# Attention bias rows loaded earlier into four tiles, and zero fills moved to middle units

## The chip, the core and the metric

The kernel runs on one core of a Trainium2 chip. It drives five engines: PE (matmuls, with its weight loads PEld), DVE (vector), ACT (scalar), POOL (GpSimd) and SP, which here issues nearly all transfers in program order; 16 DMA engines carry them. The metric is the device time of one execution in microseconds (us), the median of several runs.

## The reference

Three stages in float32: attention with a bias that depends on the distance of two positions, a gated feed-forward layer, and a layer of eight experts of which each token goes to one.

```python
# attention: batch 2, 8 heads, 576 positions, 64 per head
scores = scale * np.matmul(q, k.transpose(0, 1, 3, 2))
x = (psi_rel / psi_i)[..., None]          # log1p(|i-j|) / log1p(max(i,1))
bias = np.maximum(x @ w1 + b1, 0.0) @ w2  # hidden 32, one bias per head
scores = scores + bias.transpose(2, 0, 1)[None]
scores = scores - np.max(scores, axis=-1, keepdims=True)
attn = np.exp(scores); attn = attn / (np.sum(attn, -1, keepdims=True) + 1e-09)
x = np.matmul(attn, v)                    # then reshaped to 1152 x 512
# feed-forward: 512 -> 1536 -> 512
x = (silu(x @ w_gate) * (x @ w_val)) @ w_out
# experts: argmax routing, at most 288 tokens each, 512 -> 1024 -> 512
y = np.maximum(disp @ w1, 0.0) @ w2
out[i] = gate_w[i] * y[expert_idx[i], pos[i]]
```

## The kernel before

The attention part works in 36 *units*. The 576 query rows are cut into four chunks of 128, taken from the middle outwards, and one of 64 at the end. Each full chunk c has eight units, one for each pair of heads p and batch b, with b the fastest; the last chunk has four (units 32 to 35), one for each pair of heads, with the 64 rows of both batches side by side. One unit makes the scores of two heads ("halves"): PE multiplies queries and keys into the PSUM tile `ps_s` (line L189); DVE adds the bias and takes the row minimum of the negated sum in one instruction per half (L206, "softmax" below); ACT takes the exponential (L214); POOL adds a small number to the sums (L220), DVE inverts them (L223), POOL normalises (L227); PE transposes the weights (L256 and L262), ACT and DVE copy them out of PSUM (L267, L272, L274); PE multiplies with the values (L286), and ACT and DVE split the result into a high and a low part (L302, L304). These steps are spread over four turns of one loop: turn u does unit u's softmax, most of unit u-1's transposes, unit u-3's value product, and the scores of unit u+1. Within a turn their order is a written list (`ORDER`; `LATE` from turn 25, `TAIL` from turn 35).

The bias is made on the chip in groups of 16 query rows. DVE makes the clipped distances `bt` (L110), PE multiplies them (L128), ACT scales the result into `bo` (L146, L153), and SP stores it to the DRAM tensor `bias_d` (L157). Eleven groups are made ahead of the loop; turn u makes group 11+u (counted in the order in which the chunks are taken), until turn 24. In turns 13 to 16 and 21 to 24 a piece of that product is put in the unused half of a bank of the current unit's first score tile (`MR`), as soon as the softmax has read it.

`load_bias` (L162) fetches the bias of one chunk and one pair of heads from `bias_d` into an SBUF tile `bias_sb`: three transfers (L168 to L170), or six for the last chunk, whose rows are fetched once for each batch. A tile serves the two batches of one pair, so two units; in the last chunk it serves one. There are three such tiles in turn. The loads are issued at the head of a turn (`loads`); a load must wait until the stores of the rows that it reads have landed and until the units that used its tile are through their softmax.

SP issues everything in program order, and an instruction that waits holds all behind it. At the head of a turn stand the loads of bias, keys, values and queries, then raw weights for the next layer (turns 18 to 22), then zero fills; the group's store comes late in the turn, after ACT has written it. The zero fills are 12 transfers that clear the dispatch buffer (9 of them, `disp`) and the output (3), both in DRAM, from one SBUF tile `zero`, which POOL sets to zero once (`late["idle"]`, L603). They are issued one per turn by `late["zero"]` (L520). The feed-forward layer after the attention begins in the last three turns.

Of the kernel before, what the change touches and what calls it, by code (L numbers as in the profile page):

```python
# [10 lines left out]
F32 = mybir.dt.float32  # L11
# [26 lines left out]
LEAD = 11  # L38
IDLE = (26, 12)
RAW0 = 18  # L40
JOB0 = 25
GEO0 = 400


def attention(tc, ident, shape, qd, kd, vd, wb, geo, xh, xl, late):
    nc = tc.nc
    B, H, S, D = shape
    P = 128
# [14 lines left out]
    with ExitStack() as ctx:  # L63
        cst = ctx.enter_context(tc.tile_pool(name="a_cst", bufs=1, side="right"))
        io = ctx.enter_context(tc.tile_pool(name="a_io", bufs=2, side="right"))
# [21 lines left out]
        def load_k(b, p):  # L87
            nc.sync.dma_start(kst[:, b * NP + p], kd[b * NP + p])

        def load_v(p):  # L90
            nc.sync.dma_start(vn[:, p].rearrange("p b c d -> p (b c d)"), vd[:, p])
# [3 lines left out]
        def load_q(t):  # L95
            qst[t] = io.tile([P, NP, P], F32, tag="qst", name="qst", bufs=5)
            nc.sync.dma_start(qst[t].rearrange("p h i -> p (h i)"), qd[t])
# [61 lines left out]
        bias_sb = {}  # L159

        def load_bias(c, p):
            t = io.tile([P, 2, S], F32, tag="bias", name="bias_sb", bufs=3)  # L162
            for i0, p0, n in ([(c * P, 0, P)] if c < NF else [(c * P, 0, LO), (c * P, LO, LO)]):
                def rows(j, j0, w):
                    w_ = H * PITCH - 1
                    o = i0 * w_ + I16 - 1 + (2 * p + j) * PITCH + j0
                    return bd[o:o + n * w_].rearrange("(i w) -> i w", w=w_)[:, :w]
                nc.sync.dma_start(t[p0:p0 + n, 0, :], rows(0, 0, S))  # L168
                nc.sync.dma_start(t[p0:p0 + n, 1, LO:], rows(1, 0, NF * P))
                nc.sync.dma_start(t[p0:p0 + n, 1, :LO], rows(1, NF * P, LO))  # L170
            bias_sb[c, p] = t

        order = sorted(range(NF), key=lambda c: abs(2 * c + 1 - NT_))
        units = [(c, p, b) for c in order for p in range(NP) for b in range(B)]
# [37 lines left out]
        def exp(u, j):  # L212
            e, (mn, sm) = e_t[u], st_t[u]
            nc.scalar.activation(  # L214
                e[:, j, :], e[:, j, :], AF.Exp, bias=mn[:, j:j + 1], scale=-1.0, accum_out=sm[:, j:j + 1]
            )
# [8 lines left out]
        def normalise(u, j):  # L225
            e, rs = e_t[u], rs_t[u][:, j:j + 1]
            nc.gpsimd.tensor_scalar(e[:, j, :], e[:, j, :], rs, 1.0, ALU.mult, ALU.mult)  # L227
# [36 lines left out]
        def t_evac(u, part):  # L264
            et, ps = et_t[u], tp_t[u, part]
            if part == 2:
                nc.scalar.copy(et[:, (NB_ - 1) * P:], ps)  # L267
                return
            dst = et[:, :(NB_ - 1) * P].rearrange("p (n i) -> p n i", i=P)[:, :, part * HP:(part + 1) * HP]
            src = ps.rearrange("p (n i) -> p n i", i=HP)  # L270
            if part == 1:
                nc.vector.tensor_copy(dst, src)  # L272
            else:
                nc.scalar.copy(dst, src)  # L274
# [40 lines left out]
        def early_raw(n, h):  # L315
            r = io.tile([P, S], F32, tag="knat", name="raw0", bufs=4)[:, :512].bitcast(I32)
            late["load"](n, h, r)
            raw0.append((n, h, r))

        def early_steps(n, h, r):  # L320
            t, g = (wk.tile([P, S], F32, tag="bt", name="dec0", bufs=12)[:, :256] for _ in range(2))
            spare.append([*zip("ADDDDAD", late["decode"](n, h, r, t.bitcast(I32), g))])
# [20 lines left out]
        with tc.manual_schedule():  # L343
# [47 lines left out]
            def loads(u):  # L391
                qc = order[u // 8 + 1] * B if u // 8 < NF else None
                for x in range(3, NU):
                    if units[x][2] in (0, None) and u == max(x - 2, x // 8 * 8 - 1, 0):
                        load_bias(*units[x][:2])
                if u + 4 < len(korder):
                    load_k(*korder[u + 4])
                if u % 2 == 0 and 0 < u // 2 + 1 < NP:
                    load_v(u // 2 + 1)
                if u % 4 == 0 and qc is not None:  # L400
                    load_q(qc + u % 8 // 4)

            for u in range(NU + 2):
                if u < NU:
                    loads(u)
                if u in (RAW0, RAW0 + 1):
                    for h in range(2):
                        early_raw(u - RAW0, h)
                if u in (RAW0 + 2, RAW0 + 4):
                    late["load1"]((u - RAW0) // 2 - 1)  # L410
                if u == RAW0 + 4:
                    late["idle"]()
                if u > RAW0 + 4:
                    late["zero"]()
                if u == NU - 1:
                    dec1 = [late["decode1"](n, *(
                        wk.tile([P, S], F32, tag="bt", name="dec1", bufs=12)[:, :512].bitcast(d) for d in (I32, F32)
                    )) for n in range(2)]
                if u == JOB0:
                    for x in raw0:  # L420
                        early_steps(*x)
                R, ahead = (groups[n] if n < NG else None for n in (LEAD + u, LEAD + u + 1))
                todo = [] if ahead is None else list(range(4))

                steps = {
                    "T": (1, transposes),
                    "T9": (1, transpose_last),
                    "V0": (1, lambda v: t_evac(v, 0)),
                    "V1": (1, lambda v: t_evac(v, 1)),
                    "V2": (1, lambda v: t_evac(v, 2)),  # L430
                    "S0": (0, lambda v: softmax(v, 0)),
                    "S1": (0, lambda v: softmax(v, 1)),
                    "E0": (0, lambda v: exp(v, 0)),
                    "E1": (0, lambda v: exp(v, 1)),
                    "A": (0, add_eps),
                    "R": (0, recip),
                    "N0": (1, lambda v: normalise(v, 0)),
                    "N1": (1, lambda v: normalise(v, 1)),
                    "AV": (2, av),
                    "Q": (-1, qk),  # L440
                    "XH": (2, lambda v: evac(v, 0)),
                    "XL": (2, lambda v: evac(v, 1)),
                }
                bias = {
                    "MR": lambda: bias_mm(R, 1, {1: s_ps[u, 0][:, 1, HS:]}),
                    "M": lambda: bias_mm(R, 0),
                    "BE": lambda: bias_evac(R, 0),
                    "BR": lambda: bias_evac(R, 1),
                }
                for name in TAIL[u - NU + 1] if u >= NU - 1 else LATE if R is None else ORDER:  # L450
                    if name == "B":
                        if todo:
                            t4 = todo.pop(0)
                            bias_t4(ahead, t4, t4 + 1)
                    elif name in ("JD", "JA"):
                        job(u, name[1])
                    elif name == "JJ":
                        turn = NU
                        while any(spare):
                            job(turn, "D")  # L460
                            job(turn, "A")
                            turn += 1
                    elif name in ("K0", "K1"):
                        dec1[int(name[1])].pop(0)()
                    elif name in ("G0", "G1"):
                        gate0(int(name[1]))
                    elif name == "ACT":
                        nc.scalar.activation(ncst, ncst, AF.Sigmoid)
                    elif name in bias:
                        if R is not None:  # L470
                            bias[name]()
                    else:
                        name, _, back = name.partition(":")
                        default, step = steps[name]
                        v = u - int(back or default)
                        if 0 <= v < NU and (name, v) not in ran:
                            ran.add((name, v))
                            step(v)
                if u == NU + 1:
                    late["act"]((psg[0], psg[1]), wk.tile([P, S], F32, tag="bt", name="sg0", bufs=12))  # L480
                    for steps in dec1:
                        for step in steps:
                            step()
# [943 lines left out]
```

## Time and profile before

| | |
|---|---|
| median of 3 runs (lowest, highest) | 529.27 us (528.96 to 529.32) |
| the profiled execution | 528.89 us, of which the span is 527.2 us |
| attention, from the start to the last units | about 0 to 165 us of the span |
| PE busy, share of the span | 501.4 us, 95% |
| DVE busy | 370.1 us, 70% |
| ACT busy | 267.6 us, 51% |
| POOL busy | 104.0 us, 20% |
| HBM traffic over the span | 169 GB/s mean |

The span is what the profiler recorded from the first to the last instruction. Busy time of PE counts modelled ends of pipelined matmuls, so a busy PE may still be waited for or waiting in small parts; idle time that a row gives in brackets, with the releaser behind an arrow, is time in which the engine had nothing that it could start. The granted clock is the part of TensorE's full clock that the chip gave in a stretch. DMA share is the mean busy share of the 16 DMA engines; it can pass 1.00 a little in a short stretch. The slices of the page (40 of 13.2 us each) look like this over the attention part, the first 13 digits of each line:

```
PE   7999999999997
DVE  6899999997976
DMA  7896645779974
```

### The profile page before, as it was taken

The numbers are of one execution on the slowest core, as the hardware profiler recorded it, in microseconds if no ns is written. First come the engines' busy times: TensorE is split into PE (matmuls) and PEld (weight loads), VectorE is DVE, ScalarE is ACT, GpSimd is POOL, SyncE is SP. The second block draws the span as 40 slices with busy tenths as digits, with TensorE's granted clock in tenths as the row PEclk, the third lists the DMA queues.
The fourth block names the chain that finished last, engine by engine and source line by source line (L and its number), as shares of the span: only waits on it lengthen the run. The fifth ranks groups of instructions, "written<-read, shape, count | busy, mean of one in ns | idle before, by whom it ended". The sixth has DMA issues, their size and how long they took to land. (4 is left out here: it accounts for less than half of the span.)

```text
span 527.2 us, 11901 instructions
## 1 busy us (share of the span) xinstructions
PE 501.4 (95%) x4348; PEld 412.5 (78%) x4348; DVE 370.1 (70%) x931; ACT 267.6 (51%) x583; POOL 104.0 (20%) x218
## 2 busy tenths in 40 slices
PE   7999999999997999999999999999999599999685
PEld 4467666667767999978999889999777588897554
DVE  6899999997976899996799827643456555646221
ACT  5798889898865445453633203522323254437200
POOL 1055444444551100000000000000032210602213
PEclk9999999999998999999999999999999699999999
DMA  7896645779974754353231000000016699936720
GB/s 256 282 366 229 199 139 180 234 225 327 284 225 151 245 202 145 110 192 113 80 121 40 2 0 1 1 1 1 0 51 241 240 365 404 375 122 208 261 109 9
DMA packets 49937, 88.82 MB, mean 168 GB/s; under 512 B 7954, under 2 KB 27412, under 8 KB 49856
## 3 DMA queue, kind: packets, MB, share of 16 engines
q1 hardware_dynamic: 48416, 84.78, 47.7%
q0 software_dynamic: 1296, 3.03, 1.5%
q8 instruction: 40, 0.66, 0.5%
q14 instruction: 41, 0.34, 0.2%
q10 hardware_dynamic: 144, 0.02, 0.0%
HBM read 66.73 MB, written 22.15 MB: 169 GB/s over the span
## 5 line engine op out<-in xcount | busy, mean ns | idle before, releaser
L566 PE MATMUL ps_gv<-xh,hl 128*128 128x384 f32 x528 | 135.0, 336 | 0.0
L566 PEld LDWEIGHTS ps_gv<-xh,hl 128*128 128x128 f32 x528 | 95.5, 188 | 0.1
L566 PE MATMUL ps_gv<-xl,hl 128*128 128x384 f32 x264 | 88.7, 336 | 0.0
L859 PE MATMUL ps_o<-hl,hh 128*128 128x512 f32 x216 | 73.0, 404 | 0.2 <-ACT y L864 0.2
L214 ACT ACTIVATE e_sb<-e_sb,mn 128x576 f32<-128x576 f32 x72 | 55.4, 771 | 5.6 <-DVE mn L206 5.2
L206 DVE CUSTOM_DVE_ANT_0 e_sb<-ps_s,bias_sb 128x576 f32<-128x576 f32 x72 | 52.0, 754 | 8.8 <-DMA bias_sb<-bias_d 6.3
L227 POOL TENSOR_SCALAR e_sb<-e_sb,rs 128x576 f32<-128x576 f32 x72 | 55.2, 778 | 13.3 <-DVE rs L223 12.9
L110 DVE TENSOR_SCALAR bt<-geo_sb 128x320 f32<-128x320 f32 (+17 forms) x144 | 57.4, 439 | 0.0
L650 POOL DMA_INDIRECT disp<-y,rsi x9 | 9.0, 999 | 223.8 <-DVE rs L807 207.3
L566 PEld LDWEIGHTS ps_gv<-xl,hl 128*128 128x128 f32 x264 | 49.6, 188 | 0.1
L859 PEld LDWEIGHTS ps_o<-hl,hh 128*128 128x128 f32 x216 | 40.6, 188 | 10.4 <-issue 1.4
L286 PE MATMUL ps_x<-et,vn 128*64 128x128 f32 (+1 forms) x800 | 48.4, 271 | 0.2
L189 PE MATMUL ps_s<-kst,qst 64*128 64x288 f32 (+1 forms) x320 | 45.9, 426 | 0.0
L286 PEld LDWEIGHTS ps_x<-et,vn 128*64 128x64 f32 x800 | 40.2, 141 | 3.4 <-DVE xl L304 0.4
L576 ACT CAST hh<-sg 128x384 fp32r<-128x384 f32 x36 | 18.4, 511 | 47.7 <-DVE sg L575 47.7
L859 PE MATMUL ps_o<-hl,hlo 128*128 128x512 f32 x105 | 42.0, 400 | 0.0
L549 ACT CAST hl<-dg 128x512 fp32r<-128x512 f32 x32 | 19.1, 620 | 39.5 <-PE ps_o L859 21.6
L189 PEld LDWEIGHTS ps_s<-kst,qst 64*128 64x128 f32 (+1 forms) x320 | 24.8, 175 | 10.5 <-DVE mn L206 1.4
L256 PEld LDWEIGHTS ps_t<-ident,e_sb 64*128 64x128 f32 x576 | 24.3, 141 | 9.4 <-DVE et L272 3.1
L575 DVE TENSOR_TENSOR sg<-ps_gv,sg 128x384 f32<-128x384 f32 x35 | 19.4, 553 | 12.6 <-PE ps_gv L566 12.6
L256 PE MATMUL ps_t<-ident,e_sb 64*128 64x64 f32 x576 | 25.3, 225 | 3.0 <-DVE et L272 3.0
L274 ACT COPY et<-ps_t 128x512 f32<-128x512 f32 x36 | 21.1, 586 | 12.6 <-PE ps_t L256 12.6
(227 smaller groups left out, 913.0 us busy)
## 6 DMA issues: line engine op xcount, KB each, us to landing
eraw<-e SPq DMA_DIRECT2D x24, 512.0 KB, 9.2
bias_d<-bo SPq DMA_DIRECT2D x36, 295.5 KB, 2.6
raw<-e SPq DMA_DIRECT2D x16, 512.0 KB, 8.0
raw<-wo SPq DMA_DIRECT2D x12, 512.0 KB, 4.1
raw<-wg SPq DMA_DIRECT2D x11, 512.0 KB, 3.6
raw<-wv SPq DMA_DIRECT2D x11, 512.0 KB
disp<-zero SPq DMA_DIRECT2D x9, 520.0 KB, 3.8
bias_sb<-bias_d SPq DMA_DIRECT2D x16, 288.0 KB, 5.3
```

The source lines that it names most:

```text
L110: nc.vector.tensor_scalar(t[:, :m], dist_sb[:, :m], nbp[:, r:r + 1], None, ALU.max)
L189: nc.tensor.matmul(pss[j][i, half, :HS], qst[c * B + bb][d, p, i], kst[d, bb * NP + p, half * HS:(half + 1) * HS], start=True, stop=True, ...
L206: nc.vector.tensor_tensor_reduce(out=e[:, j, :].rearrange("p (a n) -> p a n", a=2), in0=ps[:, :, :HS], in1=bias_sb[c, p][:, j, :].rearrang ...
L214: nc.scalar.activation(e[:, j, :], e[:, j, :], AF.Exp, bias=mn[:, j:j + 1], scale=-1.0, accum_out=sm[:, j:j + 1])
L227: nc.gpsimd.tensor_scalar(e[:, j, :], e[:, j, :], rs, 1.0, ALU.mult, ALU.mult)
L256: nc.tensor.transpose(tp_t[u, h][:, n * HP:(n + 1) * HP], e[r, n * P:(n + 1) * P], ident[r, r])
L274: nc.scalar.copy(dst, src)
L286: nc.tensor.matmul(ps[j * D:(j + 1) * D, o:o + n], vn[:, p, bb, jc, j * D:(j + 1) * D], et[:, t0:t0 + n], start=jc == NF, stop=jc == NF - ...
L549: lambda: nc.scalar.copy(dh, g),
L566: nc.tensor.matmul(ps[:, :TN], w_[:, n, kc, :], x_[:, kc, t * TN:(t + 1) * TN], start=i == 0, stop=i == 3 * KC - 1,)
L575: nc.vector.tensor_tensor(sg, pss[1][:, :TN], sg, ALU.mult)
L859: nc.tensor.matmul(ps, ht_cols(f, a, tg), wot[f][b_], start=i == 0, stop=i == len(ops) - 1)
```

## The change

Two things, both in the order in which SP issues, and one in memory:

- The bias tiles are four in place of three, and the load for unit x is issued in turn max(x-3, x//8\*8-3, 0) in place of max(x-2, x//8\*8-1, 0). So loads come one turn earlier; the first of each chunk (units 8, 16, 24 and 32) comes two turns earlier, in turns 5, 13, 21 and 29, which for the first three is the turn straight after the last row group that it reads was made.
- The zero memset goes from turn 22 to turn 8, and the twelve zero fills from turns 23 to 34 to turns 9 to 20.

```diff
+ZERO0 = 8
...
-            t = io.tile([P, 2, S], F32, tag="bias", name="bias_sb", bufs=3)
+            t = io.tile([P, 2, S], F32, tag="bias", name="bias_sb", bufs=4)
...
-                    if units[x][2] in (0, None) and u == max(x - 2, x // 8 * 8 - 1, 0):
+                    if units[x][2] in (0, None) and u == max(x - 3, x // 8 * 8 - 3, 0):
                         load_bias(*units[x][:2])
...
-                if u == RAW0 + 4:
+                if u == ZERO0:
                     late["idle"]()
-                if u > RAW0 + 4:
+                if u > ZERO0:
                     late["zero"]()
```

On SP, in turns 20 to 23, the order before is this. The names are those of the tiles with a running number; `raw` is a raw weight tile, `bias_d <- bo` the store of one row group, `bias_sb_2014` the tile for units 24 and 25.

```order
L97 DMA qst_1791<-qd 128x512
L559 DMA raw0_79<-wg 128x4x256
L157 DMA bias_d_113<-bo_1832 128x591
L157 DMA bias_d_113<-bo_1895 128x591
L559 DMA raw1_80<-wv 128x4x256
L157 DMA bias_d_113<-bo_1970 128x591
L168 DMA bias_sb_2014<-bias_d_113 128x576
L169 DMA bias_sb_2014<-bias_d_113 128x512
L170 DMA bias_sb_2014<-bias_d_113 128x64
L520 DMA disp_65<-zero_66 128x4x260
```

And now, in turns 20 to 22; here the tile for units 24 and 25 is `bias_sb_1877`.

```order
L98 DMA qst_1803<-qd 128x512
L560 DMA raw0_79<-wg 128x4x256
L521 DMA out_0_dram<-zero_66 128x6x256
L158 DMA bias_d_113<-bo_1845 128x591
L169 DMA bias_sb_1877<-bias_d_113 128x576
L170 DMA bias_sb_1877<-bias_d_113 128x512
L171 DMA bias_sb_1877<-bias_d_113 128x64
L158 DMA bias_d_113<-bo_1912 128x591
L560 DMA raw1_80<-wv 128x4x256
L158 DMA bias_d_113<-bo_1986 128x591
```

The load now stands straight behind the store of the last row group that it reads, ahead of two more stores and a raw weight load, and the last output fill stands ahead of that store.

On SP in the late turns, before: from the load for units 30 and 31 (`bias_sb_2343`) to the first half of that for unit 32 (`bias_sb_2517`).

```order
L168 DMA bias_sb_2343<-bias_d_113 128x576
L169 DMA bias_sb_2343<-bias_d_113 128x512
L170 DMA bias_sb_2343<-bias_d_113 128x64
L97 DMA qst_2347<-qd 128x512
L520 DMA disp_65<-zero_66 128x4x260 x3
L168 DMA bias_sb_2517<-bias_d_113 64x576
L169 DMA bias_sb_2517<-bias_d_113 64x512
L170 DMA bias_sb_2517<-bias_d_113 64x64
```

And now, the same piece (`bias_sb_2296` and `bias_sb_2412`):

```order
L169 DMA bias_sb_2296<-bias_d_113 128x576
L170 DMA bias_sb_2296<-bias_d_113 128x512
L171 DMA bias_sb_2296<-bias_d_113 128x64
L98 DMA qst_2354<-qd 128x512
L169 DMA bias_sb_2412<-bias_d_113 64x576
L170 DMA bias_sb_2412<-bias_d_113 64x512
L171 DMA bias_sb_2412<-bias_d_113 64x64
```

No fill stands between the late loads any more. The order on PE, DVE and ACT is the same before and after; on POOL only the memset has moved.

## Rows read from the trace of the kernel before

**Rows 1.** The list of waits on DVE: engine, line, releaser, us in total, times, longest.

```profile
DVE e_sb L206 <- DMA bias_sb<-bias_d: 6.3, 6, 2.2
```

**Rows 2.** The timeline of DVE: start us, us, instruction, idle before it and its releaser.

```profile
52.02 0.76 DVE L206 CUSTOM_DVE_ANT_0 e_sb<-ps_s,bias_sb 128x576 f32<-128x576 f32 x1 [0.59 <-DMA bias_sb<-bias_d]
...
86.19 0.76 DVE L206 CUSTOM_DVE_ANT_0 e_sb<-ps_s,bias_sb 128x576 f32<-128x576 f32 x1 [0.36 <-DMA bias_sb<-bias_d]
...
118.64 0.76 DVE L206 CUSTOM_DVE_ANT_0 e_sb<-ps_s,bias_sb 128x576 f32<-128x576 f32 x1 [0.23 <-PE ps_s L189]
...
142.92 0.75 DVE L206 CUSTOM_DVE_ANT_0 e_sb<-ps_s,bias_sb 128x576 f32<-128x576 f32 x1
...
152.84 0.76 DVE L206 CUSTOM_DVE_ANT_0 e_sb<-ps_s,bias_sb 128x576 f32<-128x576 f32 x1 [1.03 <-DMA bias_sb<-bias_d]
...
158.39 0.76 DVE L206 CUSTOM_DVE_ANT_0 e_sb<-ps_s,bias_sb 128x576 f32<-128x576 f32 x1 [2.16 <-DMA bias_sb<-bias_d]
...
159.67 0.76 DVE L206 CUSTOM_DVE_ANT_0 e_sb<-ps_s,bias_sb 128x576 f32<-128x576 f32 x1 [0.52 <-DMA bias_sb<-bias_d]
```

**Rows 3.** The timeline of PE, units 7 to 9, 24 and the last ones.

```profile
46.41 1.24 PE L189 MATMUL ps_s<-kst,qst 64*128 64x288 f32 x8
...
50.44 1.24 PE L189 MATMUL ps_s<-kst,qst 64*128 64x288 f32 x8
...
54.49 1.24 PE L189 MATMUL ps_s<-kst,qst 64*128 64x288 f32 x8
...
120.17 0.32 PE L128 MATMUL ps_s<-bt,wb_sb 128*32 128x64 f32 x8
...
156.29 1.39 PE L286 MATMUL ps_x<-et,vn 128*64 128x64 f32 x40
...
161.10 1.12 PE L256 MATMUL ps_t<-ident,e_sb 64*128 64x64 f32 x15 [2.97 <-DVE et L272]
162.18 2.29 PE L286 MATMUL ps_x<-et,vn 128*64 128x64 f32 x40
...
165.16 0.33 PE L262 MATMUL ps_x<-ident,e_sb 128*128 128x128 f32 x1
```

**Rows 4.** Busy time by stretch: PE, PEld, DVE, ACT, POOL, then clock, DMA share, GB/s.

```profile
52.00:96.00 44.00, 43.94 (x596) 28.75 (x592) 41.50 (x112) 38.53 (x94) 19.85 (x32) 1.00 0.52 165
96.00:108.00 12.00, 12.00 (x169) 8.21 (x167) 11.37 (x32) 10.26 (x27) 6.00 (x9) 1.00 0.88 280
120.00:150.00 30.00, 30.00 (x443) 22.78 (x437) 26.13 (x74) 25.37 (x69) 15.03 (x27) 1.00 0.98 289
156.00:160.00 4.00, 2.02 (x48) 1.55 (x44) 1.32 (x4) 1.34 (x3) 1.47 (x2) 1.00 0.88 262
160.00:164.00 4.00, 2.90 (x49) 2.75 (x51) 3.02 (x9) 2.79 (x9) 2.13 (x3) 0.60 0.64 216
```

**Rows 5.** The timeline of POOL, the zero memset and the last normalisation.

```profile
109.35 0.31 POOL L603 MEMSET zero<- 128x260 f32 x1
...
162.09 1.92 POOL L227 TENSOR_SCALAR e_sb<-e_sb,rs 128x576 f32<-128x576 f32 x2 [0.37 <-DVE rs L223]
```

**Rows 6.** The timeline of SP: one bias row store, the last bias load's ends.

```profile
106.23 4.27 SPq L157 DMA_DIRECT2D bias_d<-bo  x2
...
152.06 0.49 SPq L168 DMA_DIRECT2D bias_sb<-bias_d  x1
...
155.95 0.59 SPq L170 DMA_DIRECT2D bias_sb<-bias_d  x1
```

**Rows 7.** DMA issues: count, KB each, median us to landing.

```profile
disp<-zero SPq DMA_DIRECT2D x9, 520.0 KB, 3.8
...
out_dram<-zero SPq DMA_DIRECT2D x3, 768.0 KB
```

**Rows 8.** Bias row stores, line L157, all 36.

```profile
DMA to landing us min/median/max: 2.1/2.6/4.8
```

**Rows 9.** Bias loads, tile bias_sb, all units.

```profile
DMA to landing us min/median/max: 3.3/4.5/7.3
```

## The prediction

> **What bounds the kernel now.** I began with the list of waits on DVE, looking for the transfer that the change moves: DVE's softmax instruction waits for a bias load six times, 6.3 us in all [rows 1]. Six waits in 72 instructions say nothing yet of the end; what matters is which of them PE feels, since PE is busy 43.94 of 44.00 us through the middle units [rows 4]. So I read DVE's timeline for where the waits lie, and PE's timeline beside it.
>
> One of the six is in unit 0, ahead of every moved instruction, and stays. Two lie at the first unit of a row chunk: 0.59 us in unit 8 and 0.36 in unit 16 [rows 2]. PE shows no trace of the first: the score products follow one another at 46.41, 50.44 and 54.49, steps of 4.03 and 4.05, with DVE's wait at 52.02 between the last two [rows 3]. The one in unit 16 is smaller. I count both at nothing; their sum, 0.95, stays as a bound.
>
> The other three are in the last two units: 1.03 in unit 34 and 2.16 and 0.52 before the two halves of unit 35 [rows 2]. There PE stands still: the transposes at 161.10 follow 2.97 us of idle, released by a copy that stands behind unit 35's softmax in DVE's order [rows 3]. [...] The slow clock has its own price: 40 value products take 2.29 us at 162.18, and 1.39 at 156.29 [rows 3].
>
> **The change part by part.** *Loads one unit earlier, with a fourth tile.* In the last units there are no bias stores left to pace SP; a load is held by its tile, by earlier transfers and by SP's own pace. Unit 35's six transfers are issued from 152.06 to 155.95 and 0.59 more, 4.5 us, and land too late [rows 6]. After the change this load needs the tile that unit 31 frees. That unit's second half starts at 142.92 and takes 0.75 [rows 2], so the load can start near 143.7, ends its issue near 148.2, and with the median landing of 4.5 us is there at 152.7 [rows 9]. Wanted it is at 158.39 - 2.16 - 1.03 = 155.20. That is 2.5 us to spare; with the worst landing, 7.3, it would be 0.3 late. Earlier loads have more room. So all three waits go: 1.03 + 2.16 + 0.52 = 3.71 us, and they lie one behind the other on the chain that ends at 161.10 on PE.
>
> *The clock.* Without the 2.97 us of idle I expect no drop, so the value products at 162.18 take 1.39 in place of 2.29: 0.90 more, since the next steps wait for their result. The sum is 4.61. What is late next is POOL: the last unit's normalisation ends at 162.09 + 1.92 = 164.01 [rows 5] and moves by the 3.71 alone, so the last transposes cannot follow the whole 0.90. I keep 0.2 of it back: 4.4.
>
> *The zero memset,* one POOL instruction of 0.31 us, goes from unit 22 to unit 8. Before, it fits the gap of 0.37 between POOL's two steps of a unit, in which POOL waits for DVE's reciprocal [rows 5]. The same gap is in unit 8; without it the price would be 0.31 on POOL, which has idle time in every unit. Nothing.
>
> *The twelve zero fills* leave units 23 to 34 for units 9 to 20. Nine carry 520 KB and three 768 KB [rows 7]. In the stretch that they fill now the DMA engines move 289 GB/s at a share of 0.98, so 295 GB/s full [rows 4]; a small fill costs 1.8 us of all engines, a large one 2.7. From 52 to 96 the share is 0.52, 22.9 us of 44; nine small fills add 16.2 and it fits. From 96 to 108 it is 0.88, 10.6 of 12, because four raw weight loads and the first decode tile are there already; three large fills add 8.0, and 6.6 us too much is left at the end. The overhang itself hides behind compute, except where something waits for it.
>
> *The wait that the change adds* is there: the load for unit 24 is now issued in unit 21, straight behind the store of the last row that it reads, and SP must hold it until that store has landed. Behind it on SP stand two stores and a raw load, none of them wanted within two units. The store is issued at 106.23 [rows 6]; by then the overhang is about 9.0 + 8.0 - 10.2 = 6.8. With the median store, 2.6 [rows 8], it lands near 115.6, and the load, at its median 4.5 [rows 9], near 120.1. Unit 24's softmax starts at 118.64 and takes 0.76; PE next needs its score bank at 120.17 [rows 2, 3], so 0.77 is free and PE would lose 0.7. At the shortest landing, 3.3, on queues that have just run empty, it loses nothing; at the worst two landings, 4.8 and 7.3, the load is there at 125.1 and PE loses 5.7. I take 0.3, near the median rows, and keep 0 and 5.7 as ends. The same turn at units 8 and 16 has no overhang before it; I count it at nothing.
>
> [...]
>
> *The early loads,* for units 4 and 6, go ahead of key and value loads, a few transfers later each; no such load is waited for on PE before. Nothing.
>
> The sum: 3.71 + 0.90 - 0.2 - 0.3 = 4.1. The profiled execution took 528.89 us, 527.2 of it span; less 4.1 that is 524.8. The median of the runs is 529.27, 0.38 above it, so I forecast 525.2.
>
> **The rivals.** *The waits go, but unit 24 pays more.* For it: the overhang is worked out, not seen, and falls on a round trip of store and load. Against: fills read one small tile, and the queues' share has stood above 0.9 for 30 us without a wait of DVE [rows 2, 4]. If PE loses 1 to 4 there, the middle 2.5, the gain is 4.4 - 2.5 and the time 527.4. [...]
>
> *Slower, by the same turn at its worst.* If both landings are as long as the longest seen, PE loses 5.7, more than the 4.4 gained; the time is 529.27 + 1.3 = 530.6. It is slower from the point where unit 24's softmax starts after 118.64 + 0.77 + 4.4 + 1.06 = 124.9. Against it: SP holds back all transfers while it waits, so the load meets empty queues.
>
> *The change doesn't do what it says.* If SP, or the tile that unit 31 frees, holds unit 35's load as long as before, the stall of the last two units stays, and so does the clock's drop: 529.3. For it: six transfers for 64 rows each take SP 4.5 us, more than a late unit. Against: the fills that stood among them are gone.
>
> **How the numbers follow.** The forecast's case gets 0.72, the milder loss at unit 24 0.15, the load that stays late 0.06, the slower case 0.07. The forecast's own range is 523.9 to 526.2: 0.3 more from no loss at unit 24 and 0.95 from units 8 and 16 on one side, the clock's 0.90 and some of POOL's lag not returned on the other. The range for 8 in 10 reaches to the milder rival: 523.9 to 527.6. A difference under 0.2%, 1.06 us, is not told from none here. Faster takes the forecast, nearly all of the milder rival and a part of the third: 0.88; the same 0.06; slower 0.06.
>
> **What would show it.** The waits of DVE for bias loads are down to the one in unit 0, and perhaps one in unit 24; PE has no idle of 3 us before the last units' transposes, and the clock stays at 1.00 there; the value products of unit 33 take 1.39 us. The DMA share from 120 to 150 falls well under 0.98, and that from 96 to 108 stands near 1. A softmax in unit 24 that starts over 1 us later than a unit's step allows shows the added turn. The forecast is wrong if PE's late units are no shorter, or if what they gain is lost again before the gate products end.

## The result and the profile after

The changed kernel takes 524.48 us, the median of 8 runs (522.87 to 527.29), against 530.76 for the kernel before in the same comparison (8 runs, 528.96 to 535.62): a ratio of 0.9878, 95% interval 0.9842 to 0.9915. The forecast was 525.2 with a range of 523.9 to 527.6. The profiled execution took 524.16 us, 522.5 of it span, 4.73 less than the profiled one of before.

The list of DVE's waits over the attention part, which answers to [rows 1], has one entry for a bias load left (total us, number, longest), the one in unit 0:

```profile
DVE e_sb L207 <- DMA bias_sb<-bias_d: 1.7, 1, 1.7
```

PE's timeline of the last units in the kernel after, against [rows 3] (start, duration, line and operation; in brackets the idle time before it):

```profile
156.64 0.33 PE L263 MATMUL ps_x<-ident,e_sb 128*128 128x128 f32 x1
...
158.45 1.39 PE L287 MATMUL ps_x<-et,vn 128*64 128x64 f32 x40 [0.51 <-DVE xl L305]
159.77 1.03 PE L257 MATMUL ps_t<-ident,e_sb 64*128 64x64 f32 x16
160.73 0.33 PE L263 MATMUL ps_x<-ident,e_sb 128*128 128x128 f32 x1
```

The row of 160.73 is the one that stood at 165.16: PE is 4.43 us earlier at the end of attention. The 2.97 us of idle are gone and 40 value products take 1.39 everywhere. The stretches of [rows 4] now read (PE, PEld, DVE, ACT, POOL busy, granted clock, DMA share, GB/s):

```profile
52.00:96.00 44.00, 44.00 (x597) 28.80 (x593) 41.50 (x112) 38.28 (x94) 19.89 (x32) 1.00 0.88 284
96.00:108.00 12.00, 12.00 (x171) 8.19 (x167) 11.37 (x32) 10.26 (x27) 5.98 (x9) 1.00 1.02 351
120.00:150.00 30.00, 30.00 (x439) 22.78 (x437) 25.82 (x74) 25.37 (x69) 15.12 (x27) 1.00 0.65 184
156.00:160.00 4.00, 3.42 (x88) 2.89 (x85) 3.15 (x9) 3.45 (x11) 2.37 (x4) 1.00 0.01 2
160.00:164.00 4.00, 3.90 (x59) 3.45 (x57) 3.30 (x6) 2.98 (x6) 0.28 (x1) 1.00 0.02 5
```

The granted clock is 1.00 in all five stretches, also from 160 to 164. The fills moved as forecast, but with the fills among the weight loads full queues carry 351 / 1.02 = 344 GB/s here, not the 295 that the prediction took from the stretch 120 to 150.

SP's queue at the two places the prediction priced, against [rows 6]: the store that unit 24's load waits for and that load, then the first and the last of unit 35's six transfers.

```profile
106.08 0.34 SPq L158 DMA_DIRECT2D bias_d<-bo  x1
113.57 0.33 SPq L169 DMA_DIRECT2D bias_sb<-bias_d  x1
...
143.55 0.45 SPq L169 DMA_DIRECT2D bias_sb<-bias_d  x1
...
146.60 0.59 SPq L171 DMA_DIRECT2D bias_sb<-bias_d  x1
```

The store landed 7.4 us after its issue. By then the queues had run empty, as the stretch from 113.4 to 114 shows (columns as above: DMA share 0.00), and the load's first transfer landed 2.8 us after its issue, near 116.4. Unit 24's softmax then starts without a wait (no bracket). That stretch, then DVE's timeline:

```profile
113.40:114.00 0.60, 0.60 (x9) 0.40 (x8) 0.57 (x3) 0.60 (x3) 0.24 (x1) 1.00 0.00 0
118.39 0.76 DVE L207 CUSTOM_DVE_ANT_0 e_sb<-ps_s,bias_sb 128x576 f32<-128x576 f32 x1
```

**Behind the attention the two profiles differ in a way that the prediction did not foresee.** At the last routing matmul (`ps_c`) 4.15 us are still there; the first matmul of the expert stage (`ps_warm`) has only 1.45. Before:

```profile
410.97 0.57 PE L872 MATMUL ps_c<-cum,ones 128*128 128x8 f32 x2
415.45 5.19 PE L1303 MATMUL ps_warm<-ident 128*128 128x128 f32 x24 [3.90 <-issue]
```

After:

```profile
406.82 0.57 PE L873 MATMUL ps_c<-cum,ones 128*128 128x8 f32 x2
414.00 5.17 PE L1304 MATMUL ps_warm<-ident 128*128 128x128 f32 x24 [6.61 <-DVE hl L538]
```

PE is idle for 2.71 us more. The releaser named cannot be the cause: before, `ps_warm` starts at 415.45, ahead of the same DVE instruction (L537, 416.89). Near the end 2.95 us come back, at the shared matmuls of the last experts. Before (timeline, then the stretch with its granted clock):

```profile
498.31 5.36 PE L1110 MATMUL ps_sh<-raw,xt 128*64 128x256 f32 x32 [3.49 <-DVEq L1333]
498.30:503.60 5.30, 5.29 (x32) 3.63 (x32) 0.42 (x1) 0.00 (x0) 0.00 (x0) 0.68 0.99 389
```

After:

```profile
495.20 3.67 PE L1111 MATMUL ps_sh<-raw,xt 128*64 128x256 f32 x32 [2.23 <-DVEq L1334]
495.20:498.80 3.60, 3.60 (x32) 2.62 (x32) 0.42 (x1) 0.00 (x0) 0.39 (x1) 1.00 0.97 346
```

The same 32 matmuls take 1.69 us more at a granted clock of 0.68, and the idle time before them is 1.26 longer. So the pair of profiles adds up as 4.15 - 2.71 + 2.95 = 4.39 of the 4.73 seen. Whether the last two terms belong to the change was the question for the experiments, beside which half of the change does what.

### The profile page after: what moved, and what is told of

Read it like the earlier page. It is cut to its first block, busy times and chain, and to the rows that moved or that the text cites. A ratio compares the mean times of both kernels' runs of the same rounds, so it can differ in the third digit from the quotient of the medians.

```text
span 522.5 us, 11900 instructions
## 1 busy us (share of the span) xinstructions
PE 497.6 (95%) x4348; PEld 410.3 (79%) x4348; DVE 370.7 (71%) x931; ACT 266.6 (51%) x583; POOL 103.3 (20%) x218
## 5 line engine op out<-in xcount | busy, mean ns | idle before, releaser
L576 DVE TENSOR_TENSOR sg<-ps_gv,sg 128x384 f32<-128x384 f32 x35 | 19.4, 553 | 12.6 <-PE ps_gv L567 12.6
L575 DVE TENSOR_TENSOR sg<-ps_gv,sg 128x384 f32<-128x384 f32 x35 | 19.4, 553 | 10.7 <-ACT sg L574 10.4
```

What stands on the lines that cost most here:

```text
L575: nc.vector.tensor_tensor(sg, pss[0][:, :TN], sg, ALU.mult)
L576: nc.vector.tensor_tensor(sg, pss[1][:, :TN], sg, ALU.mult)
```

## The experiments

Each was timed beside the kernel before on the same chip, in three groups. The medians of the kernel before were 529.68 us (22 runs; either half alone, the whole change again, the clock), 530.18 (23 runs; the crowded fills, the kernel before once more, the 32-column blocks) and 529.60 (23 runs; the runs on the number of tiles, the 64-column blocks).

**Which half.** *The loads and the tile alone,* the fills left in units 23 to 34:

```diff
 (on the kernel before)
-name="bias_sb", bufs=3)            +name="bias_sb", bufs=4)
-max(x - 2, x // 8 * 8 - 1, 0)      +max(x - 3, x // 8 * 8 - 3, 0)
```

> Loads one unit earlier and four tiles, the zero fills left in units 23 to 34. Theory A (the late stall comes from too many transfers in SP's late units, fills and bias loads together; each half of the change takes some of that away): unit 34 no longer waits, unit 35 still waits 0.5 to 2 us, since nine small fills still stand ahead of its load; 2 to 4 us faster than before. Theory B (the earlier load and the fourth tile are the cause, the fills are beside the point): all of the gain, 4.4 us or more, no wait of DVE in units 34 and 35. Theory C (the fills alone are the cause): under 1 us, the waits of 1.0 and 2.7 us stay.

524.40 us (6 runs), ratio 0.9896 (0.9848 to 0.9943). The list of DVE's waits has again only unit 0's:

```profile
DVE e_sb L206 <- DMA bias_sb<-bias_d: 2.7, 1, 2.7
```

Theory A's remaining wait in unit 35 isn't there: this is theory B's outcome.

*The fills alone,* with the old loads and three tiles:

```diff
 (on the changed kernel)
-name="bias_sb", bufs=4)            +name="bias_sb", bufs=3)
-max(x - 3, x // 8 * 8 - 3, 0)      +max(x - 2, x // 8 * 8 - 1, 0)
```

> The zero fills in units 9 to 20, loads and three tiles as before. Theory A: without the fills SP issues unit 35's six transfers from about 147 to 151, they land near 155, so no wait over 0.5 us in units 34 and 35, and the gain is that of the whole change, 4.0 to 4.7 us; the waits of 0.6 and 0.4 us in units 8 and 16 stay or grow and cost PE nothing. Theory B: under 1.5 us faster, the waits of units 34 and 35 stay. Theory C: as A, the whole gain.

526.01 us (11 runs), ratio 0.9943 (0.9907 to 0.9979). The late waits are gone too, which theory B had ruled out, but DVE waits at units 4 (0.63 us), 16 and 24. PE loses 0.55 us at unit 24, and the gain, 3.7 us by the medians, stays under the 4.0 to 4.7 of theories A and C:

```profile
87.47 0.76 DVE L207 CUSTOM_DVE_ANT_0 e_sb<-ps_s,bias_sb 128x576 f32<-128x576 f32 x1 [0.57 <-DMA bias_sb<-bias_d]
121.00 0.76 DVE L207 CUSTOM_DVE_ANT_0 e_sb<-ps_s,bias_sb 128x576 f32<-128x576 f32 x1 [1.47 <-DMA bias_sb<-bias_d]
```

Either half removes the late stall: the loads start ahead of the fills, or no fills stand among the loads. From unit 32's row on PE gains 4.28 us with the loads and the tile alone and 4.27 with the fills alone, and 4.27 with both. The two do not add up. The early loads are worth the whole gain; the fills bring nothing beside them, and alone they leave waits in the middle.

*The whole change again:*

> The whole change again, for the size: the two traces differ by 4.7 us of span (527.2 and 522.5), the medians by more. If the trace tells the whole effect, the ratio's middle lies at 0.990 to 0.992 (4.2 to 5.3 us); if there is a further 1 to 2 us outside the late units, at 0.987 to 0.988.

524.19 us (6 runs), ratio 0.9893 (0.9851 to 0.9934): between the two ranges expected, nearer to the first. PE's row of 160.73 stands at 160.69. The gap ahead of `ps_warm` is 6.50, but `ps_sh` takes 5.36 us after 3.46 of idle: that profile has the long form of both, and 524.3 of span.

**Which part of the load half.** *The changed kernel with three tiles* (`bufs=4` to `bufs=3`, nothing else):

> The changed kernel with three bias tiles in place of four; the loads still start three units ahead. In the changed kernel unit 35's six transfers start at 143.55 us, as soon as unit 31's rows have been read (VectorE's instruction of 142.76 us ends at 143.51), since unit 35 takes over that tile. With three tiles it takes over unit 32's, read at 146.55, so the six start at about 146.6 and end their issue at 150.3; with the 4.5 us of a median landing the last half is there at 154.8, against 155.14 and 155.82 at which the two halves are read. Theory T3 (the fourth tile is spare): waits of 0 to 0.5 us in unit 35, no idle spell of 3 us on PE, and the time of the changed kernel, 524.0 to 525.2 us. Rival T4 (the tile is what made the room): waits of 1 to 2.5 us in units 33 to 35, and 525.5 to 528 us.

524.56 us (6 runs), ratio 0.9895 (0.9852 to 0.9938). Unit 35's transfers start 4.4 us later than with four tiles, and 1.35 later than expected. Unit 32's rows, whose tile they take, were read by 146.89; but SP was still issuing unit 34's six until 147.53, and those had themselves waited for unit 31's rows. The half that comes last is still in time; no wait stands before it. SP's queue (the first and last of the six) and DVE's softmax of unit 35:

```profile
147.95 0.44 SPq L169 DMA_DIRECT2D bias_sb<-bias_d  x1
...
151.89 0.59 SPq L171 DMA_DIRECT2D bias_sb<-bias_d  x1
```

```profile
155.48 0.75 DVE L207 CUSTOM_DVE_ANT_0 e_sb<-ps_s,bias_sb 128x576 f32<-128x576 f32 x1
156.15 0.75 DVE L207 CUSTOM_DVE_ANT_0 e_sb<-ps_s,bias_sb 128x576 f32<-128x576 f32 x1
```

*The kernel before with four tiles* (`bufs=3` to `bufs=4`, nothing else):

> The kernel before with four bias tiles in place of three and nothing else: loads two units ahead, fills late. In the kernel before unit 35's six transfers are issued from 152.06 to 155.95 us, 5.5 us after unit 32's rows were read, so no tile held them back: they stood behind other transfers on SyncE. Theory: the tile alone does nothing; VectorE's waits of about 1.0, 2.2 and 0.5 us in units 34 and 35 stay, and the time is that of the kernel before to 0.8 us. Rival: the tile held back the transfers that stand ahead of unit 35's (those of units 33 and 34), and so delayed them all: then the waits shrink by 1 to 3.7 us and the time falls by as much.

529.27 us (12 runs), ratio 0.9982 (0.9955 to 1.0009), and the waits are all there:

```profile
153.62 0.76 DVE L206 CUSTOM_DVE_ANT_0 e_sb<-ps_s,bias_sb 128x576 f32<-128x576 f32 x1 [1.30 <-DMA bias_sb<-bias_d]
158.90 0.76 DVE L206 CUSTOM_DVE_ANT_0 e_sb<-ps_s,bias_sb 128x576 f32<-128x576 f32 x1 [1.88 <-DMA bias_sb<-bias_d]
160.22 0.76 DVE L206 CUSTOM_DVE_ANT_0 e_sb<-ps_s,bias_sb 128x576 f32<-128x576 f32 x1 [0.56 <-DMA bias_sb<-bias_d]
```

The fourth tile is spare. What counts is the turn in which the load stands on SP.

**The price of unit 24's turn.** The changed kernel with its fills crowded towards it:

```diff
-ZERO0 = 8                          +ZERO0 = 11
                 if u > ZERO0:
                     late["zero"]()
+                    if 18 <= u <= 20:
+                        late["zero"]()
```

> The changed kernel with the same twelve zero fills crowded towards unit 24: one a turn in turns 12 to 17 and two a turn in turns 18 to 20, in place of one a turn in turns 9 to 20. Three fills of 520 KB leave turns 9 to 11, so about 1.56 MB more stand ahead of the bias store of turn 20; at the 344 GB/s that the changed kernel moved in 96 to 108 us that is 4.5 us. The theory of the prediction (unit 24's rows have a small margin, and what passes it costs PE most of itself): unit 24's loads are issued at about 118 us in place of 113.57, VectorE waits 3.5 to 4.5 us there, PE loses 2 to 3.5 us by the end of attention, and the kernel takes 526.4 to 528 us; the late stall stays away. Rival: the margin in unit 24 is large or the transfers queue in another way, and the wait is under 1 us with the time at 524.0 to 525.

528.96 us (12 runs), ratio 0.9978 (0.9949 to 1.0007). SP's queue and DVE's timeline:

```profile
119.18 0.34 SPq L169 DMA_DIRECT2D bias_sb<-bias_d  x1
```

```profile
122.17 0.76 DVE L207 CUSTOM_DVE_ANT_0 e_sb<-ps_s,bias_sb 128x576 f32<-128x576 f32 x1 [3.90 <-DMA bias_sb<-bias_d]
130.13 0.76 DVE L207 CUSTOM_DVE_ANT_0 e_sb<-ps_s,bias_sb 128x576 f32<-128x576 f32 x1 [0.40 <-DMA bias_sb<-bias_d]
```

The load goes out 5.61 us later than in the changed kernel, DVE waits 3.90, PE loses 2.98 at unit 24 and 0.34 after the wait in unit 26. The trace is as expected; the median, some 4.5 above the changed kernel's, is 1 us over the range, in runs that spread from 524.6 to 531.6. So 1.7 us of the 5.61 were cover, and of the 4.30 of waits PE paid 3.32: a few fills moved towards that turn give back most of the gain.

**The clock by itself.** The kernel before with 12 idle matmuls of 128 columns in PE's stall of the last unit (they compute nothing):

```diff
-... R XH:3 JA JD XL:3 T JJ         +... R XH:3 JA JD XL:3 W T JJ
+                    elif name == "W":
+                        keep_warm(12, P)
```

> The kernel before with 12 dummy matmuls of 128x128 in the last-but-one turn, just where PE stands still for 3 us; nothing else is changed, and their result is not used. DVE's waits stay at 1.0, 2.2 and 0.5 us. If the granted clock falls because of the idle, it now stays at 1.00 from 160 to 164, the 40 value products take 1.39 us in place of 2.29, and 0.5 to 0.9 us comes back. If the clock is not a matter of that idle, nothing changes.

526.46 us (12 runs), ratio 0.9928 (0.9898 to 0.9957). DVE's waits stay (1.15, 2.02, 0.55). PE's timeline, and the stretch that had a granted clock of 0.60 in the kernel before:

```profile
158.29 2.84 PE L339 MATMUL ps_idle<-ident 128*128 128x128 f32 x24
...
162.58 1.39 PE L286 MATMUL ps_x<-et,vn 128*64 128x64 f32 x40 [0.37 <-DVE xl L304]
...
164.85 0.33 PE L262 MATMUL ps_x<-ident,e_sb 128*128 128x128 f32 x1
160.00:164.00 4.00, 3.46 (x69) 3.00 (x69) 3.34 (x9) 3.07 (x9) 1.72 (x3) 1.00 0.74 252
```

The granted clock is 1.00 and the value products take 1.39 in place of 2.29. The last row is 0.31 early though the start-up of this run was 0.53 late: 0.84 gained counted from there, 0.71 counted from unit 32's row. That is the clock's part of the gain. But the median fell by 3.2. In this profile the gap ahead of `ps_warm` is 3.35 us, and so it led to the next question.

**The gap ahead of `ps_warm`.** Two queues of the trace are marked "instruction". One of them, q8, carries 40 packets, 0.66 MB together, in the kernel before. It sent one at 293.6, 322.0, 344.2 and 366.9 us, with 256, 259 and 265 records of PE between, matmuls and weight loads together. From these counts I read it as the queue that brings PE its instructions, in blocks; that is a reading, and later the spacing is less even (tile alone: 287 records from 388.3 to 415.4 us, 9 from there to 419.1). The packet ahead of `ps_warm`, in the kernel before (a window of 412 to 413, packets, MB, share) and in the one after (411 to 412):

```profile
q8 instruction: 1, 0.02, 6.3%
```

```profile
q8 instruction: 1, 0.02, 8.3%
```

Narrower windows put them at 412.8 and 411.1, 2.65 and 2.9 us ahead of `ps_warm`. In all nine profiles of kernels without extra matmuls `ps_warm` follows its packet by 2.6 to 2.9 us:

| kernel | packet after the end of `ps_c`, us | idle before `ps_warm`, us |
|---|---|---|
| before / before again / tile alone | 1.3 / 3.8 / 3.7 | 3.90 / 6.63 / 6.65 |
| after / again / three tiles | 3.7 / 3.7 / 1.4 | 6.61 / 6.50 / 3.99 |
| loads alone / fills alone / crowded | 3.7 / 3.9 / 3.7 | 6.39 / 6.48 / 6.42 |
| 12 matmuls in the stall | -3.5 | 3.35 |
| changed, 24 of 32 columns / of 64 | -3.4 / -3.6 | 3.57 / 3.38 |
| before, 24 of 32 columns / of 64 | -3.1 / -3.0 | 3.56 / 3.55 |

PE also reads the counts (`row`) ahead of `ps_warm`. They are not what is late: DVE has made them 2.4 us after the start of `ps_c` in the short gap of before and in the long one of after.

```profile
413.11 0.28 DVE L949 TENSOR_REDUCE row<-pick 128x16 int32<-128x128 f32 x1
408.96 0.29 DVE L950 TENSOR_REDUCE row<-pick 128x16 int32<-128x128 f32 x1
```

*The kernel before once more:*

> The kernel before once more, unchanged, for a second profile of it. The first had ps_warm 3.90 us after the last routing matmul and the instruction packet at 412.8, 0.6 us ahead of the row of counts; its profiled time, 528.89, lies 0.8 to 1.9 us under the medians of its runs (529.7 and 530.8). If the gap of the kernel before is as a rule that of the four others (6.4 to 6.6 us), it shows here and the profiled time is 530 to 532: then the 2.7 us that the changed kernel seemed to give back in the expert stage were never a loss of the change. If the gap is 3.9 us again (profiled 528.5 to 529.5), the changed kernel does give them back.

531.18 us (one run), and the gap is the long one:

```profile
412.69 0.51 PE L872 MATMUL ps_c<-cum,ones 128*128 128x8 f32 x2
419.83 4.43 PE L1303 MATMUL ps_warm<-ident 128*128 128x128 f32 x24 [6.63 <-ACT hl L537]
```

So the kernel before has either gap, and so has the changed kernel (the short one with three tiles): the 2.71 us were no price of the change. This profile also has attention 2.06 later at the row of 165.16, of which 0.68 comes from unit 0 and 0.86 from unit 4 (a wait of DVE of 0.99, for which the row names a copy of ACT); the changed kernel's four comparable profiles have that row at 160.69 to 161.06.

*Blocks shifted.* In the start-up PE fills a pause with 12 idle matmuls of 128 columns. More of them, narrower, put 48 more instructions ahead of all later work and, by that reading, let every block begin earlier:

```diff
-IDLE = (26, 12)                    +IDLE = (26, 24)
-keep_warm(IDLE[1], P)              +keep_warm(IDLE[1])       (32 columns)
```

On the changed kernel:

> The changed kernel with one edit in its start-up: the 12 idle matmuls of 128 columns at 20.95 us (24 records, 2.94 us) become 24 of 32 columns (48 records, estimated 2.75 us from the 52 such records that took 2.98 us). They compute nothing. The edit puts 48 more instructions on PE ahead of everything else, so that every later block of PE's instructions begins 48 instructions earlier in the work. Theory F: the first expert matmul (ps_warm) is late because PE's instruction block for it (a packet of the queue q8 instruction) lands only at 411.1 us, 2.9 us ahead of ps_warm at 414.0; in the run with 12 more matmuls on PE in the late stall that packet came at 407.7 and ps_warm 3.35 us after the last routing matmul, in place of the 6.39 to 6.61 of the four runs with a short stall. By F the packet comes ahead of the last routing matmul here, ps_warm follows it by 3.3 to 3.9 us and not 6.5, and the kernel takes 521.5 to 522.3 us in place of 524.4. Rival N: ps_warm waits for something that depends on time or on the expert's weights and not on where the blocks begin: the gap stays 6.4 to 6.6 us and the time 524.0 to 524.8.

522.01 us (6 runs), ratio 0.9834 (0.9804 to 0.9865), the gap 3.57: as theory F had it. The start-up was slower in this profile. The filling got shorter, 1.68 us in place of 2.94 (2.75 expected), the stretch behind it ran at a granted clock of 0.68, and the units are 1.41 late from then on:

```profile
20.84 1.68 PE L340 MATMUL ps_idle<-ident 128*32 128x32 f32 x48
25.00:30.00 5.00, 4.15 (x20) 2.06 (x22) 4.29 (x16) 4.16 (x10) 2.10 (x5) 0.68 1.01 361
```

On the kernel before:

> The kernel before with the same edit of the start-up's idle matmuls (48 more instructions on PE, nothing else). Theory F: the run with 12 matmuls in the late stall was 3.2 us faster by the median, of which its trace showed 0.84 in attention; the rest was the instruction block that came early. By F this kernel keeps the whole late stall (0.99 to 1.15, 2.0 to 2.2 and 0.5 us of waits on VectorE), has ps_warm 3.3 to 3.9 us after the last routing matmul and takes 526.46 + 0.84 = 527.3 us (526.5 to 528.0). Rival N: blocks are not the cause, and it takes the time of the kernel before, 529.7 to 530.8 us. A second rival: the idle matmuls of the stall gave more than 0.84 in some way that the trace did not show; then this kernel also stays at 529.7 or above.

529.82 us (12 runs), ratio 0.9983 (0.9959 to 1.0007): no gain, against theory F's 527.3. The gap is short (3.56), but its attention is 2.70 later than in the first profile of before: 0.99 from unit 0, 0.19 from unit 4, 0.96 from waits of 0.34 and 1.35 in unit 16, and the rest in the last units. By the time alone the theory fails here; this one trace shows where the gain went. It shows too that the short filling does not decide the clock: the same 48 records of 1.68 us stand here, and the stretch behind them has 1.00.

```profile
25.00:30.00 5.00, 4.02 (x37) 2.37 (x38) 4.29 (x16) 4.09 (x11) 2.01 (x4) 1.00 1.02 360
```

Nor is a late unit 0 the filling's alone. DVE's waits for bias rows there vary from execution to execution, and with an untouched start-up unit 0 came up to 0.87 late beside them (loads and tile alone, a wait of 2.73 against 1.68 in the first profile of before).

*The same with 64 columns* (`keep_warm(IDLE[1], P // 2)`), on the changed kernel:

> The changed kernel with the 12 idle matmuls of 128 columns of the start-up made 24 of 64 columns: 48 more instructions on PE as in the run with 24 of 32 columns, but a longer stretch (estimated 3.1 us, between 48 records at 0.035 and at 0.122 us each). That run took 522.01 us with the instruction packet early (gap 3.57 us) though its idle matmuls took 1.68 us where 2.94 stood, the granted clock fell to 0.68 in 25 to 30 us and its units ran 1.41 us late from unit 0 on. Theory: the clock fell since the stretch became short and narrow; here it stays at 1.00, the units keep the changed kernel's times to 0.3 us, the gap ahead of ps_warm is 3.3 to 3.9 us, and the kernel takes 520.4 to 521.6 us. Rival: any other filling costs the start-up about 1.4 us (the wait for unit 0's rows is what counts, not the clock), and it stays at 521.7 to 522.4.

521.69 us (6 runs), ratio 0.9844 (0.98 to 0.9888), the best here, 2.9 under its neighbour with three tiles in the same comparison; it falls 0.1 above the theory's range, at the edge of the rival's, so the trace has to tell them apart. PE's timeline and the stretch behind the filling:

```profile
20.95 3.01 PE L340 MATMUL ps_idle<-ident 128*64 128x64 f32 x48
25.00:30.00 5.00, 4.52 (x47) 2.48 (x48) 4.24 (x15) 4.28 (x11) 2.88 (x6) 1.00 1.02 333
411.26 5.19 PE L1304 MATMUL ps_warm<-ident 128*128 128x128 f32 x24 [3.38 <-issue]
```

The clock is whole, units keep their times to 0.2 us, the gap is short: in this execution the filling cost the start-up nothing.

On the kernel before:

> The kernel before with the same 24 idle matmuls of 64 columns. The narrow ones lost it 2.2 us on the way to unit 15 and so hid what the early packet gave (529.82 against 530.18). Theory F: as a rule the kernel before has a gap of 6.6 us ahead of ps_warm (its second profile: 6.63; the first, with 3.90, was an exception); here it has 3.3 to 3.9 with the late stall whole, and takes 527.0 to 528.2 us, 2 to 3 us under the kernel before of the same runs. Rival: the gap of the kernel before is mostly short, and it takes the same as the kernel before to 0.8 us.

527.96 us (12 runs), ratio 0.9985 (0.9952 to 1.0019). The median is in theory F's range, but the interval takes in no change, so the time decides nothing. The gap is 3.55, but unit 0 is 0.78 late at a granted clock of 1.00, and unit 16 costs its PE 1.2 us more than the first profile's:

```profile
86.15 0.76 DVE L206 CUSTOM_DVE_ANT_0 e_sb<-ps_s,bias_sb 128x576 f32<-128x576 f32 x1 [0.52 <-DMA bias_sb<-bias_d]
88.33 0.76 DVE L206 CUSTOM_DVE_ANT_0 e_sb<-ps_s,bias_sb 128x576 f32<-128x576 f32 x1 [1.42 <-DMA bias_sb<-bias_d]
```

What stays open: why the packet comes 1.3 to 1.4 us behind `ps_c` in two of nine profiles and 3.7 to 3.9 in seven, why `ps_sh` took 5.36 us in six of fourteen profiles (granted clock 0.68 in before, before again and three tiles) and 3.67 in eight (1.00 in after, tile alone and 64 columns on the changed kernel), with kernels of the old loads and of the early ones among the six and among the eight, and why the clock fell behind one filling of 32 columns and not behind the other. The idle time before `ps_sh`, 1.89 to 3.49 us, does not decide: 2.34 was followed by 5.36 us and 3.00 by 3.67. No run tried any of these.

## Why the prediction was right

- **The late waits** (3.71) and **the clock** (0.90), less 0.2 for POOL: 4.41 predicted. From unit 32's row on, PE is 4.27 earlier (165.16 - 153.45 against 160.73 - 153.29). The clock's part is 0.71 to 0.84 by the idle matmuls, with which the granted clock from 160 to 164 was 1.00 in place of 0.60, against 0.90 less 0.2. Right. Unit 35's transfers: 143.55 to 147.19 us, against 143.7 to 148.2.
- **Unit 24's added turn** (-0.3) cost nothing. The mechanism was right, its size too large, in two terms. The mix with the fills goes at 344 GB/s and not at 295, so the store landed 7.4 us after its issue (the prediction had 9.4) and the load went out at 113.57, not 115.6. And on the empty queues the load landed in 2.8 us, less than the shortest of [rows 9], not in the median 4.5: near 116.4 and not 120.1, 2 us ahead of the softmax. The 295 came from a stretch full of bias rows and fills, and was taken for a limit of the queues. That the cover is thin, and that what passes it is paid on PE, the crowded fills showed. From 400 to 408 us, where the experts' weights are read, the changed kernel's queues move 392 GB/s at a share of 1.00, so neither 295 nor 344 is a ceiling.
- **Units 8 and 16** were counted at nothing. In the profiled execution PE got 0.13 back at unit 16. In other executions of the old order early waits cost more: 0.96 and 1.2 at unit 16 (with the start-up's filling changed), and at unit 4 0.63 (tile alone, a wait of 0.75 for bias rows). All seven profiles with the old loads wait for bias rows at unit 16, and none of the seven with the early loads does at units 4, 8 or 16. One execution understated this term.
- **The memset and the early loads** cost nothing, as predicted; PE's rows agree to 0.03 us up to the wait in unit 16.
- **The base.** The profile's 528.89 and the median of three, 529.27, lay under what more runs gave (529.6 to 530.8); for the profiled execution the short gap, 2.7 us, is enough to explain that. The medians differ by 6.28 us in the first comparison and by 5.49 when the whole change was run again, where the sum had 4.1 and attention shows 4.4. The forecast is right by its terms, but that its time, 525.2, came within 0.7 us of 524.48 is in part luck: a base that was 1.5 too low made up for most of a gain that was 2.2 too small. The early waits just named are a part of that difference that traces show; the rest is not explained.
- **The rivals.** No wait at unit 24, so neither the milder loss nor the slower case; the load is not held back. The argument against the slower case, that the load meets empty queues, is what the trace shows (a DMA share of 0.00 from 113.4 to 114). A loss of the milder rival's size, 2.98 us, appears only with the crowded fills.

## What to carry to other kernels

Where transfers stand in one queue, ask which turn the late one stands in before adding a buffer: here the turn gave all and the tile nothing. Take a full-rate figure from a stretch with the same kinds of transfers (here it was 295, 344 and 392 GB/s in three stretches), and price the cover that is left, not only the wait that goes. Compare two executions stage by stage: differences of 2.7 and 2.95 us that come and go in both kernels nearly cancelled here, and second profiles of both told them from the change.

## What was not expected of the hardware

PE's idle time ahead of `ps_warm` goes with a packet of a DMA queue marked "instruction": 6.4 to 6.65 us with the packet 3.7 to 3.9 behind `ps_c`, 3.90 and 3.99 with it 1.3 and 1.4 behind, and 3.35 to 3.57 with it 3.0 to 3.6 ahead of the end of `ps_c`. I read this, with the shifted runs, as PE idling until a block of its instructions has landed; no trace shows the block itself. With 48 more instructions that compute nothing, put into a pause hundreds of us earlier, the changed kernel took 522.01 and 521.69 us, against 524.19 to 524.56 without them (with four tiles or three). The kernel before got the short gap from them too, but no gain in time clear of the noise. A filling of 48 records of 32 columns and 1.68 us was followed by a granted clock of 0.68 in one execution and of 1.00 in another, so the filling alone does not decide it; the other twelve profiles, two of them with 64 columns and 3.01 us, have 1.00 there.
